# First block's y normalised from SBUF, and eight weight decodes moved into the feed-forward

## The chip, the cores and the metric

The kernel runs on one core of one Trainium2 chip. The metric is device time in microseconds for one execution of the whole program. TensorE's instructions are shown as PE (matmul) and PEld (weight load), VectorE's as DVE, ScalarE's as ACT, GpSimd's as POOL. SP is the engine that issues the transfers.

## The reference

Three layers in a row, all in float32 at the interface. `B, H, S, D = 4, 8, 576, 64`, so there are 2304 tokens of 512 values.

```python
scores = scale * q @ k.T                    # causal by blocks of 64
attn = softmax(scores); x = attn @ v        # [4, 576, 512]

h = relu(x @ w_in); u, v = halves(h)        # 512 + 512 columns
v_n = (v - mean) / sqrt(var + 1e-6)
v_s = einsum('ts,bsd->btd', w_spatial, v_n) + b_spatial
y = (u * v_s) @ w_out                       # [4, 576, 512]

yn = (y - mean(y)) / sqrt(var(y) + 1e-6) * g_ln
out = y + relu(yn @ w_ch1) @ w_ch2          # 512 -> 2048 -> 512
```

The weights come as float64 bits and are turned into float32 on the chip.

## The kernel before, in words

The kernel has four stages. Attention comes first, with the `w_in` products woven in. Then comes the stage this study is about, here called the spatial stage, from about 283 to 434 us. The feed-forward (`w_ch1`, `w_ch2`) follows, to the end.

**Spatial stage.** `order` is a list written out by hand: 16 steps ("s", n) and 18 steps ("y", t). A step s is `spatial(n)`: for one batch and 128 of the 512 features, 28 matmuls of 288 columns into PSUM (`sps`), two multiplications by u on DVE (`gf`, L753), the split of the next operand (ACT L737, DVE L738 and L739), and then `gate`, which splits the gated values into a high part (ACT L761) and a low part (POOL L762). A step y is `y_tile(t)`: 12 matmuls of 512 columns give 128 rows of y in PSUM (`by`), ACT copies them into `ys` (L774, two buffers), and SP stores them to DRAM as `y_d` (L775). The order is s0 to s4, y0 to y3, s5 to s8, y4 to y8, s9 to s12, y9 to y12, s13 to s15, y13 to y17.

**Weights.** `jobs` holds 48 jobs while the stage runs: 32 of `w_ch1` and 16 of the first half of `w_ch2` (`w2a`). The 16 of the second half (`w2b`) are added after it. A job is one load of 256 KB into a `raw` buffer (L661, five buffers), one ACT instruction (L87) and two DVE instructions (L88, L89). `decode_jobs` runs two jobs after each s, one after each y, and four at the end of each step of the feed-forward. The ACT instruction and the first DVE one are pinned behind what was traced before them on their engine.

**The first block's y.** The feed-forward takes 768 rows (six tiles) at a time. `prepare_y(0)` loads the six tiles of `y_d` back into `yn` (L703, two buffers), takes their statistics on DVE (`normalize`: L111, L113, L115), the power on POOL (L116), scales in place on DVE (L117), turns each tile with four transposes on PE (L709) and copies them into `yT` on ACT (L711). `operands` then makes the differences `ts` (L824, three buffers) and the split operands of the up product. `STEPS` says after which s how many pieces of these two generators are traced. The up product of the first step of the feed-forward (`first = up(0)`, matmuls `hps`, L902) is begun between the last y tiles.

**Order on the engines.** Each engine, and SP, runs its instructions in order and waits at the head of its queue. That order is made when the program is built, by a scheduler that reckons with a simulated timeline; `keep_in_program_order` pins an instruction.

Of the kernel before, what the change touches and what calls it, by code (L numbers as in the profile page):

```python
# [8 lines left out]
F32 = mybir.dt.float32  # L9
F32R = mybir.dt.float32r  # L10
U32 = mybir.dt.uint32
AF = mybir.ActivationFunctionType
ALU = mybir.AluOpType
# [3 lines left out]

PLAN = {'mm': 3, 'sc': 3, 'tr': 2, 'D': 2, 'hi0': 'v', 'hi1': 's', 'klo0': 'g', 'klo1': 'g', 'qlo0': 'g', 'qlo1': 'g', 'xm0': 'g', 'xm1': 'g', 'xh0': 'g', 'xh1': 'g', 'xl0': 'g', 'xl1': 'g', 'dm': 'g', 'dh': 'g', 'ev0': 3, 'ev1': 2, 'rate': 24500.0, 'vrb': 3, 'ds': 2, 'dy': 1, 'raw': 5, 'yn': 2, 'ts': 3, 'ring': 8, 'wt': 2, 'cb': 1, 'hq': 8, 'packed': 4, 'plain': 3, 'pre': 8, 'py': 10, 'pyn': 4, 'dn0': 2, 'dnn': 4, 'vl': 'v', 'pace': 3, 'wd': 7, 'tl0': 'v', 'tl1': 'v', 'xe': 's', 'pt': 6, 'dstart': 8}  # L20


def f32(ap):
# [9 lines left out]
def tile_kernel(  # L33
# [12 lines left out]
    nc = tc.nc  # L46

    def E(k, p=None):
        k = PLAN[k if p is None else k + ("0" if p < 4 else "1")]
        return {"v": nc.vector, "g": nc.gpsimd, "s": nc.scalar}[k]  # L50

    def cp(k, p, out, src):
        e = PLAN[k if p is None else k + ("0" if p < 4 else "1")]
        if e == "v":
# [6 lines left out]
    KD = w_in.shape[1]  # L61
    DM = 128 * KD
# [3 lines left out]
    NT = NB * S  # L66
# [39 lines left out]
        MM(out_ps, lhsT=a[0], rhs=b[1], start=False, stop=False)  # L106
        MM(out_ps, lhsT=a[1], rhs=b[0], start=False, stop=last)  # L107

    def normalize(pool, x, rows=128, here=lambda ins: ins):
        st = pool.tile([128, 6], F32, tag="st", name="st")  # L110
        here(nc.vector.bn_stats(st[:rows], x[:rows]))  # L111
        mv = pool.tile([128, 2], F32, tag="mv", name="mv")
        nc.vector.bn_aggr(mv[:rows], st[:rows])  # L113
        rs = pool.tile([128, 1], F32, tag="rs", name="rs")
        nc.vector.tensor_scalar(rs[:rows], mv[:rows, 1:2], 1e-6, None, op0=ALU.add)  # L115
        nc.gpsimd.tensor_tensor(rs[:rows], rs[:rows], nhalf[:rows], op=ALU.pow)  # L116
        return lambda: nc.vector.tensor_scalar(  # L117
            x[:rows], x[:rows], mv[:rows, 0:1], rs[:rows], op0=ALU.subtract, op1=ALU.mult
        )


# [3 lines left out]
    at = tc.alloc_tile_pool(name="at", bufs=2, side="right")  # L125
    p_mm = tc.alloc_tile_pool(name="p_mm", bufs=PLAN["mm"], space=PSUM, side="left")
    p_sc = tc.alloc_tile_pool(name="p_sc", bufs=PLAN["sc"], space=PSUM, side="right")
    p_tr = tc.alloc_tile_pool(name="p_tr", bufs=PLAN["tr"], space=PSUM, side="right")

# [4 lines left out]

    PACKED = PLAN['packed']
    nat = {}
# [27 lines left out]
    idn = const.tile([128, 128], F32, name="idn")  # L164
# [6 lines left out]
    g_sb = const.tile([128, KD], F32, name="g_sb")  # L171
# [327 lines left out]
    def chain(*gens):  # L499
        for g in gens:  # L500
            if g is not None:
                yield from g
# [8 lines left out]
    D = PLAN['D']  # L511
    for u in range(NS + 8):
        p, i = divmod(u, NU)
# [24 lines left out]
        else:  # L538
            b, k = divmod(u, NU * NP)
# [102 lines left out]
    fy = tc.alloc_tile_pool(name="fy", bufs=2, side="left", reuse_waits="tile")  # L642
    fb = tc.alloc_tile_pool(name="fb", bufs=1, side="left", reuse_waits="tile")
    p_h = tc.alloc_tile_pool(name="p_h", bufs=2, space=PSUM, side="left", reuse_waits="tile")
# [5 lines left out]
    jobs = []  # L650
# [12 lines left out]

    done = [0]

    def decode_jobs(k):
        for _ in range(k):
            i = done[0]
            if i == len(jobs):
                return  # L670
            done[0] += 1
            if i not in raws:
                fetch_raw()
            raw = raws.pop(i)
            m = dc.tile([128, 256], F32, tag="dm", name="dm")
            decode(raw, m, raw[:, :, 0], jobs[i][1], tc.keep_in_program_order)
            fetch_raw()
# [9 lines left out]
    NTB = 6  # L687
    BLK = NTB * 128
    HB = BLK // 2
    NBLK = NT // BLK  # L690
    of = out.rearrange("b s d -> (b s) d")
    yT = fy.tile([128, KD, BLK], F32, name="yT", bufs=1)

    def prepare_y(blk):
        if blk >= NBLK:
            return
        yn_t = {}

        def fetch(t):
            if t < NTB:  # L700
                r0 = blk * BLK + 128 * t
                yn_t[t] = fy.tile([128, DM], F32, tag="yn", name="yn", bufs=PLAN["yn"])
                nc.sync.dma_start(out=yn_t[t], in_=y_d[r0:r0 + 128, :])  # L703

        def flip(t):
            yn = yn_t.pop(t)
            tr = p_h.tile([128, 512], F32, tag="h", name="ytr")
            for kc in range(KD):
                nc.tensor.transpose(tr[:, 128 * kc:128 * kc + 128], yn[:, 128 * kc:128 * kc + 128], idn)  # L709
            for kc in range(KD):  # L710
                nc.scalar.activation(  # L711
                    yT[:, kc, 128 * t:128 * t + 128], tr[:, 128 * kc:128 * kc + 128], AF.Copy, scale=g_sb[:, kc:kc + 1]
                )
            fetch(t + 2)

        fetch(0)
        fetch(1)
        yield
        for t in range(NTB):
            scale = normalize(fy, yn_t[t], here=tc.keep_in_program_order) if blk else normalize(fy, yn_t[t])  # L720
            yield
            scale()
            yield
            if t > 0:
                flip(t - 1)
                yield
        flip(NTB - 1)
        yield

# [35 lines left out]

    split_vn(0)

    def y_tile(t):
        c0 = 128 * (t % 9)
        ps = p_by.tile([128, DM], F32, tag="by", name="by")  # L770
        for kc in range(KF):
            mm3(ps, [g[:, kc, c0:c0 + 128] for g in gt], [w[:, kc, :] for w in wo], kc == 0, kc == KF - 1)
        ys = fy.tile([128, DM], F32, tag="ys", name="ys")
        nc.scalar.copy(ys, ps)  # L774
        nc.sync.dma_start(out=y_d[128 * t:128 * t + 128, :], in_=ys)  # L775

    seq = []
    for b in range(NB):
        seq += [("s", KF * b + fc) for fc in range(KF)]
        t0 = 9 * (b // 2) + (0 if b % 2 == 0 else 4)  # L780
        ys = [("y", t) for t in range(t0, t0 + (4 if b % 2 == 0 else 5))]
# [30 lines left out]
    def operands(first=False):  # L812


        b11, b12, b21, b22 = (yT[:, 2 * i:2 * i + 2, HB * k:HB * k + HB] for i in range(2) for k in range(2))
        t1, t2, t3 = (fb.tile([128, KD // 2, HB], F32, tag="ts", name="ts", bufs=3) for _ in range(3))

        def put(i, src):
            pool = fb if i in (0, 2, 6) else fr if i == 4 else fl
            b_t[i] = [pool.tile([128, KD // 2, HB], F32R, tag=f"b{i}{x}", name=f"b{i}{x}") for x in "hl"]  # L820
            split(src, *b_t[i], "s", "v" if i % 2 else "g")

        def sub(out, x, y):
            nc.vector.tensor_tensor(out, x, y, op=ALU.subtract)  # L824

        put(0, b11)
        yield
        put(2, b21)
        if first:
            yield  # L830
            put(6, b22)
            yield
        sub(t1, b12, b11)
        sub(t2, b22, t1)
        yield
        if first:
            sub(t3, b22, b12)
            yield
        put(1, t2)
        if not first:  # L840
            sub(t3, b22, b12)
            yield
        put(3, t3)
        sub(t2, b21, t2)
        yield
        put(5, t2)
        yield
        put(4, t1)
        yield
        if not first:  # L850
            put(6, b22)
            yield
# [117 lines left out]
        nc.sync.dma_start(out=of[r0:r0 + 128, :], in_=yr)  # L970


    STEPS = {6: 1, 7: 2, 8: 2, 9: 3, 10: 3, 11: 3, 12: 3, 13: 2, 14: 3, 15: 2}
    ahead = chain(prepare_y(0), operands(True))
    gate = None
    for kind, n in order:
        if kind == "s":
            gate = spatial(n)
            if n % (2 * KF):
                gate()  # L980
                gate = None
            decode_jobs(PLAN['ds'])
            for _ in range(STEPS.get(n, 0)):
                next(ahead)
            if n == NB * KF - 1:
                p_b1.release()
                ss.release()
                fl = tc.alloc_tile_pool(name="fl", bufs=1, side="left", reuse_waits="tile")
                for _ in range(2):
                    next(ahead)  # L990
                weights(0)
                first = up(0)
        else:
            y_tile(n)
            decode_jobs(PLAN['dy'])
            if n >= NT // 128 - 4 and n < NT // 128 - 1:
                next(first)
        if gate is not None and (kind == "y" or n == 0):
            gate()
            gate = None  # L1000
# [17 lines left out]
    for n, (blk, m) in enumerate(pairs):  # L1018
# [18 lines left out]
        for k in (2, 1, 2, 2, 1, 2, 2):  # L1037
# [3 lines left out]
            for _ in range(k):  # L1041
                t = next(lower)
# [3 lines left out]
        for _ in upper:  # L1046
            pass
        del h_t[n]
        decode_jobs(PLAN["dnn"])
        for i in range(2):  # L1050
            if n + 1 < len(pairs):
# [67 lines left out]
```

## Time and profile before

| | us |
|---|---|
| median of 3 runs | 823.11 (822.58 to 824.65) |
| the profiled execution, its own time | 824.04 |
| its span in the profile | 822.3 |
| PE busy in the span | 791.5 (96%) |
| DVE busy | 519.7 (63%) |
| chain that ended last: share of PE, of DMA, of DVE | 75%, 9%, 8% |

The span is what the trace covers; the 1.7 us beside it lie ahead of the first and behind the last instruction shown. PE is busy nearly always, so what can be won lies where PE sits idle or runs at a lower clock. In the tables a row names the line of the kernel, the engine, the operation, and output<-input by the names of the program.

### The profile page before, as it was taken

Reading aid. Unit: us, or ns where it says so; the run is one execution under the profiler, and the core shown is the slowest. Engines: PE = TensorE matmul, PEld = TensorE weight load, DVE = VectorE, ACT = ScalarE, POOL = GpSimd, SP = SyncE. Lnnn points to the kernel's source line nnn. Section 1 sums busy time; section 2 is a strip of 40 time slices with the busy share of each in tenths; the row PEclk is TensorE's granted clock in tenths of the full one; section 3 lists DMA queues with packets and bytes.
Section 4 is the critical chain, followed back from the end, with each engine's and each line's share of the span. In section 5 each row is a group of like instructions: output and inputs, shape, how many; then the busy total and the mean of one; then the engine's idle time right before and its main releaser. Section 6 shows DMA issues by size and latency. Waiting matters only on the chain.

```text
span 822.3 us, 13272 instructions
## 1 busy us (share of the span) xinstructions
PE 791.5 (96%) x4480; PEld 669.7 (81%) x4480; DVE 519.7 (63%) x1179; ACT 423.9 (52%) x1071; POOL 440.2 (54%) x429
## 2 busy tenths in 40 slices
PE   7899999999999999899889999999999999999998
PEld 4567788768877889888768988898889888988986
DVE  5857654664565276656696578578556659555533
ACT  4688677666755454345554465464345445434331
POOL 4889646654553243214367545587555469445531
PEclk9999999999999999999999999999999999999999
DMA  8745535445241568778531122204000002100002
GB/s 243 199 125 160 157 123 161 137 128 156 86 153 55 162 211 274 236 255 253 203 131 65 52 90 81 61 1 154 1 13 27 14 1 75 67 1 1 1 1 77
DMA packets 54551, 90.24 MB, mean 110 GB/s; under 512 B 6866, under 2 KB 17234, under 8 KB 54484
## 3 DMA queue, kind: packets, MB, share of 16 engines
q1 hardware_dynamic: 54484, 89.40, 35.3%
q8 instruction: 35, 0.57, 0.3%
q14 instruction: 32, 0.26, 0.1%
HBM read 70.43 MB, written 18.95 MB: 109 GB/s over the span
## 4 chain that ended last, share of the span: by engine, by line
PE 75%; DMA 9%; DVE 8%; ACT 3%; SPq 2%; issue 2%; POOL 1%; ACTq 0%; DVEq 0%; POOLq 0%
PE hps L902 20%; PE o L105 8%; PE o L107 8%; PE o L106 8%; PE pv L385 6%; PE tr L332 5%; PE sc L259 3%; PE ups L105 2%; DMA raw<-in_w_in_dram 2%; PE ups L107 2%; PE ups L106 2%; DMA raw<-in_w_ch_dram 2%; DMA yn<-y_d 2%; PE vps L105 1%; PE vps L106 1%
## 5 line engine op out<-in xcount | busy, mean ns | idle before, releaser
L101 POOL TENSOR_TENSOR a<-s,a 128x256 fp32r<-128x256 f32 x96 | 77.4, 811 | 79.1 <-ACT a L96 79.1
L106 PE MATMUL o<-w,h 128*128 128x512 f32 x288 | 112.9, 393 | 0.0
L274 DVE CUSTOM_DVE_ANT_0 p<-sc,mask 128x256 f32<-128x256 f32 (+4 forms) x160 | 73.8, 472 | 56.5 <-PE tr L332 17.5
L105 PE MATMUL o<-w,h 128*128 128x512 f32 x288 | 107.7, 398 | 0.7 <-ACT h L894 0.7
L908 DVE TENSOR_TENSOR c<-hps,c 128x384 f32<-128x384 f32 x120 | 66.6, 555 | 65.4 <-PE hps L902 63.4
L281 ACT ACTIVATE p<-p,nm 128x384 f32<-128x384 f32 (+3 forms) x144 | 83.8, 583 | 32.7 <-DVE nm L274 30.0
L107 PE MATMUL o<-w,h 128*128 128x512 f32 x288 | 97.7, 397 | 1.1 <-DVE h L895 1.1
L101 POOL TENSOR_TENSOR a<-w,a 128x256 fp32r<-128x256 f32 x72 | 63.8, 888 | 40.8 <-ACT a L96 36.7
L96 ACT CAST a<-s 128x256 fp32r<-128x256 f32 x96 | 38.4, 404 | 86.4 <-PE hps L902 78.2
L332 PE MATMUL tr<-idn,p 128*128 128x128 f32 (+1 forms) x400 | 70.2, 287 | 6.1 <-DVE pH L323 5.7
L323 DVE COPY pH<-tr 128x512 f32<-128x512 f32 (+1 forms) x88 | 49.5, 572 | 25.7 <-PE tr L332 25.6
L332 PEld LDWEIGHTS tr<-idn,p 128*128 128x128 f32 (+1 forms) x400 | 47.7, 143 | 19.3 <-issue 5.7
L105 PEld LDWEIGHTS o<-w,h 128*128 128x128 f32 x288 | 53.8, 188 | 11.6 <-ACT h L894 2.1
L106 PEld LDWEIGHTS o<-w,h 128*128 128x128 f32 x288 | 54.1, 188 | 10.1
L107 PEld LDWEIGHTS o<-w,h 128*128 128x128 f32 x288 | 53.3, 188 | 9.8 <-DVE h L895 2.0
L116 POOL TENSOR_TENSOR rs<-rs,nhalf 128x1 f32<-128x1 f32 x36 | 22.8, 634 | 64.4 <-DVE rs L115 64.1
L199 POOL TENSOR_TENSOR stack<-qkt,stack 64x576 fp32r<-64x576 f32 x24 | 34.2, 1427 | 42.2 <-ACT stack L57 41.5
L895 DVE SCALAR_TENSOR_TENSOR h<-c,h 128x384 fp32r<-128x384 f32 x72 | 49.1, 704 | 1.5 <-ACT h L894 1.5
L762 POOL TENSOR_TENSOR gt<-gf,gt 128x576 fp32r<-128x576 f32 (+1 forms) x17 | 25.5, 1501 | 44.0 <-ACT gt L761 43.9
L87 ACT ACTIVATE dm<-raw 128x256 f32<-128x256 f32 (+1 forms) x76 | 34.4, 473 | 26.6 <-DVE w2b L89 6.4
L259 PE MATMUL sc<-stack 128*128 128x512 f32 (+3 forms) x192 | 45.3, 344 | 0.4 <-DVE nm L274 0.2
L96 ACT CAST a<-w 128x256 fp32r<-128x256 f32 x72 | 28.9, 403 | 27.1 <-PE hps L902 27.0
(171 smaller groups left out, 2236.6 us busy)
## 6 DMA issues: line engine op xcount, KB each, us to landing
raw<-in_w_ch_dram SPq DMA_DIRECT2D x64, 256.0 KB
qkt<-in_qk_dram SPq DMA_DIRECT2D x112, 144.0 KB
vt<-in_v_dram SPq DMA_DIRECT2D x16, 320.0 KB
rb<-r_d SPq DMA_DIRECT2D x32, 144.0 KB
u_d<-ur SPq DMA_DIRECT2D x16, 288.0 KB
us<-u_d SPq DMA_DIRECT2D x16, 288.0 KB
y_d<-ys SPq DMA_DIRECT2D x18, 256.0 KB
yn<-y_d SPq DMA_DIRECT2D x18, 256.0 KB
```

Of the source, the lines that this page charges most:

```text
L96: nc.scalar.copy(hi, src)
L101: {"v": nc.vector, "g": nc.gpsimd}[low].tensor_tensor(lo, src, f32(hi), op=ALU.subtract)
L105: MM(out_ps, lhsT=a[0], rhs=b[0], start=first, stop=False)
L106: MM(out_ps, lhsT=a[0], rhs=b[1], start=False, stop=False)
L107: MM(out_ps, lhsT=a[1], rhs=b[0], start=False, stop=last)
L259: MM(s_ps[:, :nn], lhsT=st[:, j, i, q], rhs=st[:, j, 2, 0:nn], start=(i == 0), stop=(i == 1))
L274: nc.vector.tensor_tensor_reduce(pt[:, o:o + n], s_ps[:, :n], m, -0.125, 3e38, ALU.add, ALU.min, nm[:, i:i + 1])
L281: nc.scalar.activation(pt[:, :n], pt[:, :n], AF.Exp, bias=nm[:, 0:1], scale=-1.0, accum_out=sm[:, col:col + 1])
L323: nc.vector.tensor_copy(out, src)
L332: nc.tensor.transpose(tr[:w, o:o + 128], pt[:, 128 * kc:128 * kc + w], idn)
L902: MM(ps, lhsT=a[x], rhs=b[y], start=not more and kc == 0 and k == 0, stop=kc == KD // 2 - 1 and k == 2, skip_group_check=True,)
L908: nc.vector.tensor_tensor(out, ps, x, op=ALU.add)
```

## The change

Three edits, all around the first block.

1. `y_tile` normalises the first six tiles itself: after the copy `ys` and its store, `normalize` reads `ys` and writes a `yn` tile. The six loads from `y_d` go. `flip_y` (the transposes and the copies into `yT`) runs for tile t after y tile t+1, or after the next s.
2. The copies `ys` of tiles 0 to 12 lie in the three buffers of the differences (`ts`); tiles 13 to 17 keep the two old ones.
3. `decode_jobs` stops at 40 jobs in the spatial stage, so the last 8 jobs of `w2a` run in the feed-forward with the 16 of `w2b`. The rate there goes from 4 to 5 jobs per step.

`STEPS` now counts the pieces of `operands` alone: one after each of s11 to s15. Before, the first three of them were traced after s14, the next two after s15.

```diff
-PLAN = {... 'dnn': 4, ...}
+PLAN = {... 'dnn': 5, ...}
-    def normalize(pool, x, rows=128, here=lambda ins: ins):
+    def normalize(pool, x, rows=128, here=lambda ins: ins, out=None):
...
-            x[:rows], x[:rows], mv[:rows, 0:1], rs[:rows], op0=ALU.subtract, op1=ALU.mult
+            (x if out is None else out)[:rows], x[:rows], mv[:rows, 0:1], rs[:rows],
+            op0=ALU.subtract, op1=ALU.mult,
...
-    def decode_jobs(k):
+    def decode_jobs(k, last=1 << 30):
...
-            if i == len(jobs):
+            if i == min(len(jobs), last):
...
+    def flip_y(t, yn):
+        tr = p_h.tile([128, 512], F32, tag="h", name="ytr")
+        for kc in range(KD):
+            nc.tensor.transpose(tr[:, 128 * kc:128 * kc + 128], yn[:, 128 * kc:128 * kc + 128], idn)
+        for kc in range(KD):
+            nc.scalar.activation(
+                yT[:, kc, 128 * t:128 * t + 128], tr[:, 128 * kc:128 * kc + 128], AF.Copy, scale=g_sb[:, kc:kc + 1]
+            )
...
+    flips = []
     def y_tile(t):
...
-        ys = fy.tile([128, DM], F32, tag="ys", name="ys")
+        if t < NT // 128 - 5:
+            ys = fb.tile([128, KD // 2 * HB], F32, tag="ts", name="ys", bufs=3)[:, :DM]
+        else:
+            ys = fy.tile([128, DM], F32, tag="ys", name="ys")
         nc.scalar.copy(ys, ps)
         nc.sync.dma_start(out=y_d[128 * t:128 * t + 128, :], in_=ys)
+        if t < NTB:
+            yn = fy.tile([128, DM], F32, tag="yn", name="yn", bufs=PLAN["yn"])
+            normalize(fy, ys, out=yn)()
+            flips.append((t, yn))
...
-    STEPS = {6: 1, 7: 2, 8: 2, 9: 3, 10: 3, 11: 3, 12: 3, 13: 2, 14: 3, 15: 2}
-    ahead = chain(prepare_y(0), operands(True))
+    STEPS = {11: 1, 12: 1, 13: 1, 14: 1, 15: 1}
+    ahead = operands(True)
...
-            decode_jobs(PLAN['ds'])
+            decode_jobs(PLAN['ds'], 40)
+            while flips:
+                flip_y(*flips.pop(0))
...
             y_tile(n)
-            decode_jobs(PLAN['dy'])
+            decode_jobs(PLAN['dy'], 40)
+            while len(flips) > 1:
+                flip_y(*flips.pop(0))
```

## Rows read from the trace of the kernel before

**Rows 1.** Windows, two feed-forward steps: busy us (instructions), PEclk, DMA share, GB/s.
```profile
core 0: us, PE busy (x) PEld busy (x) DVE busy (x) ACT busy (x) POOL busy (x), PEclk, DMA share, GB/s
501.50:517.80 16.30, 16.30 (x85) 14.58 (x84) 13.32 (x27) 8.78 (x23) 8.99 (x11) 1.00 0.28 78
517.80:534.00 16.20, 16.03 (x81) 13.76 (x81) 8.62 (x14) 7.66 (x21) 7.08 (x8) 1.00 0.12 37
```
**Rows 2.** Windows over the spatial stage, as in rows 1.
```profile
309.00:337.00 28.00, 28.00 (x179) 26.08 (x178) 17.69 (x44) 12.64 (x26) 6.61 (x4) 1.00 0.90 288
337.00:347.00 10.00, 7.93 (x53) 6.98 (x53) 7.70 (x19) 3.46 (x8) 2.98 (x3) 1.00 0.64 193
347.00:372.00 25.00, 24.21 (x142) 21.50 (x142) 14.29 (x39) 12.15 (x29) 6.04 (x4) 1.00 0.79 251
372.00:404.00 32.00, 28.66 (x178) 25.42 (x177) 20.18 (x50) 14.53 (x36) 11.11 (x9) 1.00 0.65 208
404.00:434.50 30.50, 26.66 (x126) 21.65 (x125) 26.54 (x44) 17.38 (x44) 18.47 (x16) 0.94 0.52 177
```
**Rows 3.** Waits of PE, 308 to 440 us: us in total, times, longest.
```profile
PE sps L105 <- DVE gf L753: 3.1, 4, 1.4
PE ytr L709 <- DVE yn L117: 2.7, 2, 1.7
PE hps L902 <- ACT a L96: 1.4, 2, 1.2
PE by L105 <- ACT gt L761: 1.2, 1, 1.2
PE sps L105 <- DVE mv L113: 0.6, 1, 0.6
PE hps L902 <- DVE b1l L101: 0.5, 1, 0.5
```
**Rows 4.** DVE by line, 309 to 404 us: busy, mean ns | idle ahead of it.
```profile
L88 DVE TENSOR_SCALAR raw<-raw 128x256 uint32<-128x256 uint32 x40 | 12.6, 316 | 17.0 <-DMA raw<-in_w_ch_dram 17.0
L111 DVE BATCH_NORM_STATS2 st<-yn 128x6 f32<-128x512 f32 x6 | 4.2, 693 | 9.7 <-DMA yn<-y_d 9.7
L113 DVE BATCH_NORM_AGGREGATE mv<-st 128x2 f32<-128x6 f32 x6 | 1.0, 171 | 0.0
L115 DVE TENSOR_SCALAR rs<-mv 128x1 f32<-128x1 f32 x6 | 0.8, 139 | 0.0
```
**Rows 5.** Timeline, 337 to 401.5 us: start, us, engine, line [idle before <-releaser].
```profile
339.83 0.69 DVE L111 BATCH_NORM_STATS2 st<-yn 128x6 f32<-128x512 f32 x1 [1.24 <-DMA yn<-y_d]
...
341.70 0.37 PE L105 MATMUL sps<-ws,hl 128*128 128x288 f32 x1 [1.40 <-DVE gf L753]
...
386.46 1.87 POOL L101 TENSOR_TENSOR b0l<-yT,b0h 128x768 fp32r<-128x768 f32 x1 [0.19 <-ACT b0h L96]
...
386.51 2.10 DVE L117 TENSOR_SCALAR yn<-yn,mv,rs 128x512 f32<-128x512 f32 x1
...
400.30 0.55 POOL L116 TENSOR_TENSOR rs<-rs,nhalf 128x1 f32<-128x1 f32 x1 [6.28 <-DVE rs L115]
```
**Rows 6.** The chain that ended last, in order of time: start us, us, what.
```profile
332.21 4.25 DMA y_d<-ys
```
**Rows 7.** Waits of ACT, 308 to 440 us, as in rows 3.
```profile
ACT ys L774 <- DMA y_d<-ys: 6.4, 2, 3.7
```
**Rows 8.** DVE by line, 404 to 434.5 us.
```profile
L89 DVE SCALAR_TENSOR_TENSOR w2a<-dm,raw 128x256 uint32<-128x256 uint32 x10 | 5.5, 549 | 0.3
L88 DVE TENSOR_SCALAR raw<-raw 128x256 uint32<-128x256 uint32 x9 | 4.2, 471 | 1.4 <-DMA raw<-in_w_ch_dram 1.4
```
**Rows 9.** Windows over the end of the stage, as in rows 1.
```profile
418.00:420.00 2.00, 1.06 (x3) 0.48 (x3) 2.00 (x4) 1.87 (x7) 1.32 (x2) 1.00 0.51 146
420.00:422.00 2.00, 1.47 (x6) 0.97 (x6) 2.00 (x4) 1.02 (x5) 2.00 (x3) 0.78 0.36 118
422.00:424.00 2.00, 2.00 (x6) 1.90 (x7) 2.00 (x3) 2.00 (x6) 2.00 (x2) 0.50 0.31 117
```
**Rows 10.** Tiles yn, ys: duration ns min/median/max, first and last start us.
```profile
L117 DVE TENSOR_SCALAR yn<-yn,mv,rs x18: 529/547/2101, 341.7 to 641.3; 128x512 f32<-128x512 f32 x18
...
L774 ACT COPY ys<-by x18: 567/584/603, 328.1 to 434.2; 128x512 f32<-128x512 f32 x18
```
**Rows 11.** Timeline of PE: first and last of 24 matmuls of y tiles.
```profile
329.23 0.40 PE L105 MATMUL by<-wo,gt 128*128 128x512 f32 x1
...
334.46 0.39 PE L107 MATMUL by<-wo,gt 128*128 128x512 f32 x1
```
**Rows 12.** DVE by line, 434.5 to 530 us.
```profile
L89 DVE SCALAR_TENSOR_TENSOR w2b<-dm,raw 128x256 uint32<-128x256 uint32 x16 | 10.1, 629 | 0.6
L88 DVE TENSOR_SCALAR raw<-raw 128x256 uint32<-128x256 uint32 x16 | 7.9, 492 | 0.0
```

More of the change, by code (lines that the diff above doesn't have):

```diff
@@ L16 @@
 DRAM = bass.MemoryType.DRAM
-PLAN = {'mm': 3, 'sc': 3, 'tr': 2, 'D': 2, 'hi0': 'v', 'hi1': 's', 'klo0': 'g', 'klo1': 'g', 'qlo0': 'g', 'qlo1': 'g', 'xm0': 'g', 'xm1': 'g', 'xh0': 'g', 'xh1': 'g', 'xl0': 'g', 'xl1': 'g', 'dm': 'g', 'dh': 'g', 'ev0': 3, 'ev1': 2, 'rate': 24500.0, 'vrb': 3, 'ds': 2, 'dy': 1, 'raw': 5, 'yn': 2, 'ts': 3, 'ring': 8, 'wt': 2, 'cb': 1, 'hq': 8, 'packed': 4, 'plain': 3, 'pre': 8, 'py': 10, 'pyn': 4, 'dn0': 2, 'dnn': 4, 'vl': 'v', 'pace': 3, 'wd': 7, 'tl0': 'v', 'tl1': 'v', 'xe': 's', 'pt': 6, 'dstart': 8}
+PLAN = {'mm': 3, 'sc': 3, 'tr': 2, 'D': 2, 'hi0': 'v', 'hi1': 's', 'klo0': 'g', 'klo1': 'g', 'qlo0': 'g', 'qlo1': 'g', 'xm0': 'g', 'xm1': 'g', 'xh0': 'g', 'xh1': 'g', 'xl0': 'g', 'xl1': 'g', 'dm': 'g', 'dh': 'g', 'ev0': 3, 'ev1': 2, 'rate': 24500.0, 'vrb': 3, 'ds': 2, 'dy': 1, 'raw': 5, 'yn': 2, 'ts': 3, 'ring': 8, 'wt': 2, 'cb': 1, 'hq': 8, 'packed': 4, 'plain': 3, 'pre': 8, 'py': 10, 'pyn': 4, 'dn0': 2, 'dnn': 5, 'vl': 'v', 'pace': 3, 'wd': 7, 'tl0': 'v', 'tl1': 'v', 'xe': 's', 'pt': 6, 'dstart': 8}
 def f32(ap):
@@ L705, in flip @@
         def flip(t):
[L706 to L713, printed above, removed]
+            flip_y(t, yn_t.pop(t))
             fetch(t + 2)
@@ L719, in prepare_y @@
         for t in range(NTB):
-            scale = normalize(fy, yn_t[t], here=tc.keep_in_program_order) if blk else normalize(fy, yn_t[t])
+            scale = normalize(fy, yn_t[t], here=tc.keep_in_program_order)
             yield
```

## The prediction

> **What bounds the kernel now.** I first read the page: PE is busy 96% of the span, so only stretches in which PE idles or is clocked down can give anything back. The table of windows comes next, to find them. In the feed-forward there is next to nothing: a step of 16.30 us shows PE busy 16.30 [rows 1]. The spatial stage is where it lacks: 2.07 us idle in 337 to 347, 0.79 in 347 to 372, 3.34 in 372 to 404, 3.84 in 404 to 434.5 [rows 2], 10.0 us together. In the last of these the granted clock is below 1 as well, 0.94 on average; that is 0.06 x 30.5 = 1.8 us more. So about 11.8 us is all that could come back.
>
> The list of PE's waits says who ended this idle time [rows 3]: DVE, nearly always (the product `gf`, the scaled `yn`, the statistics), and ACT at the end. But DVE is busy just 14 to 20 us in those longer windows up to 404 us. It is late, not full. DVE's own idle time shows why [rows 4]: 17.0 us in front of the first decode instruction, waiting for its weights, and 9.7 us in front of the statistics, waiting for the reload of y. Both stand at the head of an in-order queue, and what PE needs stands behind. The timeline has the pattern: statistics start at 339.83 after a wait for the reload, and PE gets its `gf` with 1.40 us of idle time at 341.70 [rows 5]. After 404 us it is another story: DVE is busy 26.54 of 30.5 us, so there it is full.
>
> **The reload goes (edit 1).** It removes six loads of 256 KB and six waits at the head of DVE's queue, 9.7 us of DVE idle time. What of that PE felt: the longest wait for `gf`, 1.4, the two for `yn`, 2.7, the one for the aggregate, 0.6 [rows 3]. That makes 4.7 us, my term, **-4.7**. Lower bound of the gain 1.0: the next at DVE's head may be a decode that waits for its load instead. Upper bound 6.4, with the three other `gf` waits (3.1 - 1.4 = 1.7) as backlog of the same stalls. SP is rid of six issues that wait for a store to land, and the transfers of 1.57 MB; at the 208 GB/s of 372 to 404 [rows 2] that is 7.6 us of the transfer engines' time, which makes weight loads earlier. I give it nothing of its own, since PE doesn't wait for these loads directly; it stands against the lower bound.
>
> The work itself stays: six statistics, aggregates, additions and scales on DVE, six powers on POOL, 24 transposes, 24 ACT copies. It moves ahead, next to the y tiles.
>
> **The copies in `ts` (edit 2).** Three buffers where there were two, and each is now held until its store has landed and its scale has run. The differences are first written after s14 and need the buffers of tiles 10 to 12 back. A store took 4.25 us from issue to landing in the chain [rows 6]; the cover is s13 and s14, 56 matmuls, by 32 us for 178 PE instructions [rows 2] about 10 us, an estimate. So 0; without that cover it would be up to 4.25 us. ACT waited 6.4 us for stores to give back one of its two buffers [rows 7]; a third can only help, and I give it 0, since no wait of PE hangs on it in the list [rows 3].
>
> **Eight decodes leave the stage (edit 3).** Per job 0.549 + 0.471 us of DVE [rows 8], eight jobs 8.2 us, out of the 26.5 us that DVE is busy from 404 us on. ACT loses eight short instructions with them. The pieces of `operands` also start three s steps earlier, so the high parts are off ACT before the rush. What is to be won is the 3.84 us of idle time and the 1.8 us of clock. The windows show the clock falling to 0.50, the lower of its two levels (1.2 GHz), at 422 to 424, behind two windows with PE busy 1.06 and 1.47 of 2 us [rows 9]. Without that hole it need not fall. Not all goes: the weights' split for the first up product (ACT, POOL) still has to follow the last s. Bounds 0 and 5.7; I take **-4.0**, nearer the upper end, because the DVE time taken away (8.2) is twice the idle time.
>
> **The new waits: six flips.** PE now gets transposes of tile t behind y tile t+1. The chain from the last matmul of tile t is copy 0.58 [rows 10], statistics 0.69, aggregate 0.17, addition 0.14 [rows 4], power 0.55 [rows 5], scale 0.55 at the median, 2.10 at most [rows 10]: 2.7 to 4.2 us. The cover is the next y tile, 12 matmuls at (334.46 - 329.23)/23 = 0.227 us each [rows 11], 2.7 us. Tiles 0, 1, 2 and 4 have just that; tiles 3 and 5 also have a spatial step in front. So four flips with an excess of 0 to 1.5 us, 0 to 6.0 in all, more when ACT or DVE is held ahead of the copy or the statistics. DVE's decodes wait 17.0 us for weights [rows 4], and a statistics behind one of them delays PE. I take 0.5 each for four, **+2.0**; most scales in the trace ran at the short time, but queues are never quite empty.
>
> The scale's long time has a cause that the rows show: the one at 386.51 took 2.10 us while POOL worked on a subtraction from 386.46 for 1.87 [rows 5]. The Trainium skill, page "SBUF — State Buffer", section "Who interferes with whom", says that a tensor_scalar on VectorE can take a mode that uses the pair of ports it shares with GpSimd, and that whoever comes second is then held for the whole of the other's instruction. The trace agrees at that place. The move puts the scales beside the y tiles, where the gate's subtraction runs on POOL; by the rule each could meet one, and by the rows' median none does. By the median the four flips cost nothing, by the maximum 6.0.
>
> **The feed-forward takes the eight jobs.** There a job costs 0.629 + 0.492 = 1.12 us of DVE [rows 12]. The steps with decodes had four and get five; the fifth step had none and gets four. The fullest step had DVE busy 13.32 of 16.30 us and would come to 14.4; the fifth 8.62 and would come to 13.1 [rows 1]. PE was fully busy with DVE at 13.3, so the cover holds. **+0.5**; bounds 0 and 9.0, all eight on PE's path if the two PSUM banks of the up product gave no slack. The weights are in time: jobs 40 to 43 are split at the end of step 1 (counted from 0) and are decoded at the end of step 0, one step ahead.
>
> **Sum.** -4.7 - 4.0 + 2.0 + 0.5 = -6.2 us. From the profiled execution's 824.04 that makes 817.8. The median shown is 0.93 lower, so 816.9 for a median.
>
> **Rivals.**
> A. *The weights' loads take the reload's place.* DVE's queue still holds decodes that waited 17.0 us. If the next instruction at its head is one of those, the first term shrinks to -1.0, the second, which doesn't hang on it, to -2, and the flips cost 2: with 0.5 that is -0.5, so 822.6. For it: decodes are pinned in order. Against it: the reload's own transfers and SP's blocked issues go, so weights come earlier; and of the 17.0 us at most the 1.7 us of the other `gf` waits reached PE [rows 3, 4].
> B. *PE waits for its flips: slower.* One mechanism: the chain behind each y tile is longer than the tile that covers it. The gain ahead of it is 8.7 less 0.5, so it decides from 8.2/6 = 1.4 us per flip on, all six. At 2.1 us each (the whole length of the slow scale) 12.6 come on: +4.4, 827.5. For it: scales ran up to 2.10, and the decodes' waits can hold a statistics. Against it: only four flips are without a spatial step, and the scheduler can put a flip later.
> C. *The feed-forward pays.* Half of the 9.0 us shows: -8.7 + 2 + 4.5 = -2.2, 820.9. Against it: PE was full at 82% of DVE.
> D. *The whole stage closes up.* All 11.8 us and no flip waits: 811.3. Against it: the tail of the stage has a true chain through `gf`, `gt` and the last tiles.
>
> **How the numbers follow.** A run of this kernel tells a change from none at about 0.3%, 2.5 us. Chances: forecast 0.57 (its own range 813 to 820), A 0.15, B 0.12, C 0.08, D 0.08. Faster by over 0.3% takes the forecast, D, and a little of C and A: 0.69. Slower takes B and a small part of the mixed cases, 0.12; the rest, 0.19, is no difference. The range for 8 in 10 leaves out most of B and the edge of D: 811.5 to 823.5.
>
> **What would show it.** Right: no wait of DVE for y before the feed-forward; PE busy over 31 of 32 us in 372 to 404; the granted clock at 1.00 through the end of the stage; the first up products a few us earlier; feed-forward steps still 16.2 to 16.3 us. Wrong: a row "PE ytr waits for DVE yn" above 4 us (B), the idle time in front of the decodes grown by the same 9.7 us (A), steps of the first block above 17 us (C), or differences that wait for a store (edit 2).

## The result, and the profile after

| | before | changed |
|---|---|---|
| median, us | 822.85 (821.84 to 824.65, 4 runs) | 813.24 (812.78 to 814.33, 4 runs) |
| ratio of the runs, 95% interval | | 0.9891 (0.9874 to 0.9908) |
| profiled execution, own time / span | 824.04 / 822.3 | 812.78 / 811.0 |

The kernel got faster by 9.6 us between medians; 816.9 had been forecast, 811.5 to 823.5 as the range. First the page of the changed kernel, its span and PE's line:

```profile
span 811.0 us, 13252 instructions
...
PE 787.5 (97%) x4480; PEld 670.4 (83%) x4480; DVE 525.9 (65%) x1179; ACT 423.6 (52%) x1071; POOL 441.9 (54%) x429
```

Where in the span it came from is seen with two marks, the last matmul of `ups` and the matmuls of `o`. These are rows of tile `ups` and tile `o`, with the first and last start at the end of the numbers. Before:

```profile
L107 PE MATMUL ups<-xT,win x128: 289/294/380, 108.1 to 309.1; 128*128 128x288 f32 x128
...
L105 PE MATMUL o<-w,h x288: 387/395/501, 436.5 to 817.7; 128*128 128x512 f32 x144
```

Changed:

```profile
L107 PE MATMUL ups<-xT,win x128: 289/294/380, 107.3 to 308.4; 128*128 128x288 f32 x128
...
L105 PE MATMUL o<-w,h x288: 387/395/505, 424.9 to 806.3; 128*128 128x512 f32 x144
```

From the one mark to the other the spatial stage took 436.5 - 309.1 = 127.4 us and now takes 116.5: 10.9 us less. The feed-forward, first to last `o`, took 381.2 and takes 381.4. So nearly all of the 11.3 us between the two spans lies in the stage, and the eight extra decodes cost the feed-forward next to nothing. (These two executions lie further apart than the medians, 11.3 us against 9.6.)

The windows of the changed kernel, as in [rows 2]; the last one ends where `o` begins:

```profile
337.00:347.00 10.00, 7.48 (x55) 6.81 (x54) 8.75 (x18) 5.08 (x13) 4.55 (x4) 1.00 0.55 168
347.00:372.00 25.00, 25.00 (x147) 22.27 (x146) 17.12 (x45) 14.06 (x35) 8.40 (x6) 1.00 0.77 239
372.00:404.00 32.00, 31.76 (x199) 29.15 (x198) 23.70 (x47) 13.68 (x29) 9.84 (x6) 1.00 0.79 254
404.00:424.90 20.90, 20.49 (x105) 17.64 (x104) 14.31 (x20) 12.78 (x28) 15.14 (x15) 1.00 0.21 73
```

In 337 to 404 PE idles 2.52 + 0 + 0.24 = 2.8 us where it idled 2.07 + 0.79 + 3.34 = 6.2 [rows 2]. In the last window it idles 0.4 us at a granted clock of 1.00, where the end of the stage had 3.8 us and a clock of 0.94 [rows 2]. DVE is busy 14.3 of 20.9 us there and no longer full. PE's waits, 308 to 440 us, as in [rows 3], and DVE by line, 309 to 404 us, as in [rows 4]:

```profile
PE sps L105 <- DVE gf L756: 1.7, 2, 1.5
PE ytr L698 <- DVE yn L117: 0.6, 1, 0.6
PE sps L107 <- DVE low L741: 0.5, 1, 0.5
PE hps L915 <- ACT b4h L96: 0.4, 1, 0.4
```
```profile
L88 DVE TENSOR_SCALAR raw<-raw 128x256 uint32<-128x256 uint32 x40 | 18.3, 457 | 11.6 <-DMA raw<-in_w_ch_dram 11.6
...
L111 DVE BATCH_NORM_STATS2 st<-ys 128x6 f32<-128x512 f32 x6 | 4.1, 686 | 0.2 <-ACT ys L783 0.2
L117 DVE TENSOR_SCALAR yn<-ys,mv,rs 128x512 f32<-128x512 f32 x6 | 3.3, 546 | 3.3 <-POOL rs L116 3.2
```

The statistics' wait is gone (9.7 to 0.2 us), and the wait for weights fell too, from 17.0 to 11.6: the reload's wait did not turn into one for weights. Against that, the decodes' first instruction (L88) is busy 18.3 us where it was 12.6 [rows 4], 457 ns on average against 316. The flips cost PE 0.6 us in one place.

### The profile page after: what moved, and what is told of

Same layout as the page of the kernel before. It is cut to its first block, busy times and chain, and to the rows that moved or that the text cites. A ratio compares the mean times of both kernels' runs of the same rounds, so it can differ in the third digit from the quotient of the medians.

```text
span 811.0 us, 13252 instructions
## 1 busy us (share of the span) xinstructions
PE 787.5 (97%) x4480; PEld 670.4 (83%) x4480; DVE 525.9 (65%) x1179; ACT 423.6 (52%) x1071; POOL 441.9 (54%) x429
## 4 chain that ended last, share of the span: by engine, by line
PE 78%; DVE 8%; DMA 6%; ACT 3%; issue 2%; SPq 2%; POOL 1%; DVEq 0%; ACTq 0%; POOLq 0%
PE hps L915 20%; PE o L105 8%; PE o L107 8%; PE o L106 7%; PE pv L386 6%; PE tr L333 5%; PE sc L260 4%; DMA raw<-in_w_ch_dram 2%; PE ups L105 2%; PE ups L107 2%; PE ups L106 2%; DMA raw<-in_w_in_dram 2%; PE by L107 2%; PE by L105 2%; PE by L106 2%
```

## The experiments

Twelve kernels. Each was timed beside the kernel before on its own chip, so ratios are what is compared. A ratio's interval is some 1.0 to 1.9 us to either side. "Stage" is the time between the two marks in the profiled execution. That is one execution, and it need not be a typical one: it was the slowest of six in late_operands and the fastest of six in spare_loads_read and spare_loads_tiny.

| run | median us | ratio, 95% interval | stage us |
|---|---|---|---|
| changed kernel | 813.24 | 0.9891 (0.9874 to 0.9908) | 116.5 |
| without_decode_move | 815.12 | 0.9903 (0.9887 to 0.9918) | 119.1 |
| decode_move_alone | 822.50 | 0.9992 (0.9978 to 1.0005) | 125.4 |
| reload_kept | 821.88 | 0.9980 (0.9966 to 0.9993) | 125.8 |
| two_copy_buffers | 814.57 | 0.9899 (0.9882 to 0.9915) | 117.5 |
| late_operands | 815.42 | 0.9917 (0.9897 to 0.9936) | 119.3 |
| spare_loads | 818.69 | 0.9947 (0.9923 to 0.9970) | 122.0 |
| spare_loads_read | 815.95 | 0.9928 (0.9906 to 0.9951) | 118.5 |
| reload_five_buffers | 823.20 | 1.0005 (0.9988 to 1.0021) | 127.1 |
| spare_loads_no_wait | 811.93 | 0.9875 (0.9853 to 0.9896) | 116.5 |
| spare_loads_tiny | 815.09 | 0.9905 (0.9889 to 0.9922) | 117.7 |
| operands_pinned | 811.42 | 0.9862 (0.9844 to 0.9880) | 114.8 |
| flips_uncovered | 812.59 | 0.9893 (0.9871 to 0.9915) | 116.3 |

**First question: which of the three edits.** Four runs undo or do one alone.

without_decode_move:
```diff
-PLAN = {... 'dnn': 5, ...}
+PLAN = {... 'dnn': 4, ...}
-            decode_jobs(PLAN['ds'], 40)
+            decode_jobs(PLAN['ds'], 48)
...
-            decode_jobs(PLAN['dy'], 40)
+            decode_jobs(PLAN['dy'], 48)
```


> The changed kernel with edit 3 undone: all 48 jobs run in the spatial stage, four per step in the feed-forward. Theory (two separate parts: the reload held DVE's queue before 404 us, the decodes filled DVE after it): the end of the stage gets its idle time back, 4 to 5 us, so 817 to 818. Rival 'early operands' (the end of the stage got faster because the differences and operands were made earlier, not because decodes left): 814 or less. Rival 'decodes alone': 820 to 823.

It gave 815.12. The end of the stage did not get its 4 to 5 us back: 0.9903 against 0.9891 is 1.0 us by ratios, 1.9 by medians, with overlapping intervals, and the stage of the profiled execution is 2.6 us longer. The theory of two separate parts is wrong in its second half, and the rival "early operands" (814 or less) is closer. With all 48 jobs in the stage PE idles 2.4 us from 404 us to the first `o`, and the granted clock stays at 1.00:

```profile
404.00:427.10 23.10, 20.73 (x103) 17.25 (x103) 19.64 (x33) 14.98 (x35) 14.48 (x15) 1.00 0.44 148
```

decode_move_alone, the kernel before with
```diff
-PLAN = {... 'dnn': 4, ...}
+PLAN = {... 'dnn': 5, ...}
-    def decode_jobs(k):
+    def decode_jobs(k, last=1 << 30):
...
-            if i == len(jobs):
+            if i == min(len(jobs), last):
...
-            decode_jobs(PLAN['ds'])
+            decode_jobs(PLAN['ds'], 40)
...
-            decode_jobs(PLAN['dy'])
+            decode_jobs(PLAN['dy'], 40)
```


> The kernel before with edit 3 alone: 40 jobs in the stage, the rest at five per step of the feed-forward; y is still loaded back. Theory of two separate parts: 4 to 5 us faster than before, 818 to 819. Rival 'early operands': under 1 us, about 822. Rival 'decodes alone': near the changed kernel, 813 to 815.

It gave 822.50, a ratio whose interval holds 1; the stage of the profiled execution is 2.0 us shorter than before. With eight jobs fewer PE still idles at the end of the stage: 3.3 of 31.5 us in the window 404 to 435.5, against 4.5 of 32.5 in the same part of the kernel before (404 to 436.5). DVE is busy 24.6 of the 31.5 us and no longer full, so its fullness is not what most of PE's idle time came from. One thing differs: the granted clock is 1.00, where it was 0.95 in that part.

```profile
404.00:435.50 31.50, 28.21 (x146) 23.53 (x146) 24.61 (x34) 18.45 (x42) 19.15 (x17) 1.00 0.37 126
```

reload_kept, the same with the copies in `ts` as well (edit 2):
```diff
-        ys = fy.tile([128, DM], F32, tag="ys", name="ys")
+        if t < NT // 128 - 5:
+            ys = fb.tile([128, KD // 2 * HB], F32, tag="ts", name="ys", bufs=3)[:, :DM]
+        else:
+            ys = fy.tile([128, DM], F32, tag="ys", name="ys")
```


> Edits 2 and 3 without edit 1: copies of y in the three buffers of the differences and eight decodes moved, but y of the first block is still loaded back and normalised as before. Theory of two parts: what the reload cost stays, so 818 to 819, as with the decode move alone, the buffers giving at most 1 us. Rival 'the buffers matter': 815 to 816.

821.88, and not the 818 to 819 of two parts. From here to the changed kernel only edit 1 is missing, with its places in `STEPS`, and that step is 0.9980 to 0.9891: 7.3 of 822.85 us. The windows of reload_kept, from its first mark to 404 us and from there to the first `o`, say where:

```profile
308.00:404.00 96.00, 90.11 (x558) 81.48 (x557) 62.00 (x154) 44.45 (x100) 26.17 (x20) 1.00 0.77 243
404.00:433.80 29.80, 26.49 (x123) 21.45 (x122) 21.64 (x25) 15.38 (x37) 19.00 (x17) 0.94 0.33 115
```

Ahead of 404 us PE idles 5.9 us, against 2.8 in the changed kernel. Behind it PE idles 3.3 us, and the clock costs 0.06 x 29.8 = 1.8 us more, against 0.4 us at 1.00. So edit 1 works in both parts of the stage, and the clock is low here although the eight decodes are gone.

two_copy_buffers, the changed kernel with the four lines of edit 2 back to the one old line:
```diff
-        if t < NT // 128 - 5:
-            ys = fb.tile([128, KD // 2 * HB], F32, tag="ts", name="ys", bufs=3)[:, :DM]
-        else:
-            ys = fy.tile([128, DM], F32, tag="ys", name="ys")
+        ys = fy.tile([128, DM], F32, tag="ys", name="ys")
```


> The changed kernel with edit 2 undone: the copies of y lie in the two old buffers, each now held by its store and its scale. Theory: the buffers are worth little, 813 to 814.5. Rival 'the buffers matter' (with two, the copy of the third tile waits for a store, its PSUM bank is not free and PE waits): 816 to 819, with a wait of PE's y matmuls for the copy above 2 us.

814.57: 0.7 us by ratios, within the intervals; PE waits 0.8 us for the copy there. So the buffers are worth little, as expected (813 to 814.5).

**Second question: what in edit 1.** The timeline has a hint. The first difference (`ts`) starts at 408.51 in the kernel before and at 409.46 with the decodes moved alone; in the changed kernel it starts at 396.57, 11.9 us earlier, or 11.2 counted from the first mark (three kernels, a row each):

```profile
408.51 0.95 DVE L824 TENSOR_TENSOR ts<-yT 128x768 f32<-128x768 f32 x1
```
```profile
409.46 0.95 DVE L824 TENSOR_TENSOR ts<-yT 128x768 f32<-128x768 f32 x1
```
```profile
396.57 0.96 DVE L837 TENSOR_TENSOR ts<-yT 128x768 f32<-128x768 f32 x1 [0.37 <-DMA y_d<-ys]
```

What the late start does is seen in the kernel before. Two differences take over 2 us each on DVE, the last products `gf` stand behind them, ACT can split `gf` into `gt` only then, and PE waits 1.20 us (timeline of the kernel before):

```profile
409.75 2.26 DVE L824 TENSOR_TENSOR ts<-yT,ts 128x768 f32<-128x768 f32 x1
411.93 2.18 DVE L824 TENSOR_TENSOR ts<-yT 128x768 f32<-128x768 f32 x1
...
414.57 0.44 DVE L753 TENSOR_TENSOR gf<-us,sps 128x288 f32<-128x288 f32 x1
...
415.05 0.43 ACT L761 CAST gt<-gf 128x288 fp32r<-128x288 f32 x1 [3.80 <-DVE gf L753]
...
415.53 0.50 PE L105 MATMUL by<-wo,gt 128*128 128x512 f32 x1 [1.20 <-ACT gt L761]
```

late_operands keeps all three edits and traces the operands late again, pinned there; operands_pinned has the same pins at the changed kernel's places. The difference between the two is `STEPS` alone, but for pins on the differences (DVE), which only late_operands has.

late_operands:
```diff
-    STEPS = {11: 1, 12: 1, 13: 1, 14: 1, 15: 1}
+    STEPS = {14: 3, 15: 2}
...
-            split(src, *b_t[i], "s", "v" if i % 2 else "g")
+            hi, lo = b_t[i]
+            here = tc.keep_in_program_order if first else lambda ins: ins
+            here(nc.scalar.copy(hi, src))
+            (nc.vector if i % 2 else nc.gpsimd).tensor_tensor(lo, src, f32(hi), op=ALU.subtract)
...
-            nc.vector.tensor_tensor(out, x, y, op=ALU.subtract)
+            here = tc.keep_in_program_order if first else lambda ins: ins
+            here(nc.vector.tensor_tensor(out, x, y, op=ALU.subtract))
```


> The changed kernel with the five pieces of the operands traced where they were before (three after s14, two after s15) and their copies and differences pinned behind what was traced ahead of them; y is still normalised from its copy and eight decodes still leave the stage. Theory of lateness (most of the gain comes because the first block's y is ready some 35 us sooner, so differences and operands are made ahead of the rush at the end of the stage): 816.5 to 819, with PE idle 3 us or more from 404 us on. Rival 'head of the queue' (DVE no longer stands waiting for the reload): 813 to 814.

operands_pinned:
```diff
-            split(src, *b_t[i], "s", "v" if i % 2 else "g")
+            hi, lo = b_t[i]
+            here = tc.keep_in_program_order if first else lambda ins: ins
+            here(nc.scalar.copy(hi, src))
+            (nc.vector if i % 2 else nc.gpsimd).tensor_tensor(lo, src, f32(hi), op=ALU.subtract)
```


> The changed kernel with the ACT copies of the operands pinned at the places where they are traced (after s11 and later), so that none is run some 40 us ahead and the POOL subtraction behind it doesn't fall on DVE's decodes at 343 us. Theory (the 2.5 us that PE still idles in 337 to 347 come from that subtraction, as two decodes there took 1.54 and 1.96 us instead of 0.28): 811.5 to 812.5. Rival (PE's wait there has another cause, or moves on): 813 to 814.

815.42 and 811.42, 0.9917 and 0.9862, intervals apart: operands that are late in this way cost 4.5 us. Against the changed kernel alone late_operands is just 2.1 us up, less than expected, because its pins also help ahead of 404 us, where PE idles 1.0 us and not 2.8. The window from 404 us to the first `o` in late_operands, then in operands_pinned, then PE's longest wait of late_operands, from its list of waits:

```profile
404.00:428.60 24.60, 21.23 (x86) 17.13 (x85) 17.48 (x18) 11.44 (x25) 19.26 (x16) 0.86 0.18 65
```
```profile
404.00:424.30 20.30, 19.46 (x96) 16.45 (x96) 14.23 (x18) 12.64 (x28) 15.79 (x15) 1.00 0.23 73
```
```profile
PE by L107 <- POOL gt L765: 2.5, 1, 2.5
```

With late operands PE idles 3.4 us and the granted clock averages 0.86; with early ones 0.8 us at 1.00. Idle time and a lower clock, as in the kernel before [rows 2, 9], are back although the eight decodes are gone. But this is not the hole of the kernel before. Pinned late, three subtractions for the operands stand in POOL's queue ahead of the last `gt`, and PE waits for POOL (timeline of late_operands):

```profile
401.79 1.88 POOL L837 TENSOR_TENSOR b0l<-yT,b0h 128x768 fp32r<-128x768 f32 x1
...
403.61 2.60 POOL L837 TENSOR_TENSOR b2l<-yT,b2h 128x768 fp32r<-128x768 f32 x1
...
406.18 2.55 POOL L837 TENSOR_TENSOR b6l<-yT,b6h 128x768 fp32r<-128x768 f32 x1
...
408.69 2.44 POOL L765 TENSOR_TENSOR gt<-gf,gt 128x288 fp32r<-128x288 f32 x2
...
410.25 1.22 PE L107 MATMUL by<-wo,gt 128*128 128x512 f32 x2 [2.47 <-POOL gt L765]
```

In the kernel before two of these three subtractions had started by 388.29 us. Also, the first difference of late_operands starts 9 us later than that of operands_pinned (403.40 against 394.51), not 12. So 4.5 us shows that late operands can cost as much; it is not a measure of what lateness cost in the kernel before.

operands_pinned also answers its own question. In the changed kernel two decodes near 343 us were slow, each while POOL was at work (timeline of the changed kernel):

```profile
341.14 1.43 POOL L765 TENSOR_TENSOR gt<-gf,gt 128x576 fp32r<-128x576 f32 x1 [0.46 <-ACT gt L764]
341.19 1.54 DVE L88 TENSOR_SCALAR raw<-raw 128x256 uint32<-128x256 uint32 x1
...
343.23 2.03 POOL L101 TENSOR_TENSOR b0l<-yT,b0h 128x768 fp32r<-128x768 f32 x1 [0.66 <-ACT b0h L96]
343.45 1.96 DVE L88 TENSOR_SCALAR raw<-raw 128x256 uint32<-128x256 uint32 x1
```

With the operands pinned behind s11 the first stays slow (1.53 us at 342.05), beside `gt`. The second takes 0.28 us, PE's wait of 1.5 us for `gf` is gone, and PE is busy 9.05 of the 10 us from 337 on, not 7.48 (operands_pinned, its timeline and its window):

```profile
344.31 0.28 DVE L88 TENSOR_SCALAR raw<-raw 128x256 uint32<-128x256 uint32 x1
```
```profile
337.00:347.00 10.00, 9.05 (x68) 8.59 (x67) 8.19 (x21) 6.00 (x19) 2.52 (x3) 1.00 0.53 169
```

811.42 lies just below the expected 811.5 to 812.5 and is the fastest of the versions that do the kernel's work and no more; its interval overlaps that of the changed kernel, so the 1.8 us between the medians are not clear of noise.

**Third question: the rest of edit 1.** Taken as they stand, 4.5 of 7.3 us would leave some 3 for the waits at the head of DVE's queue, for SP's, or for the bytes. Four runs add spare loads to the changed kernel, and one gives the old reload more buffers. The spare loads are traced at the old places of the reload (s6 to s13) and write into the two old copy buffers, which are free then; nothing uses what they bring. SP issues those of spare_loads from 333 to 368 us, where it issued the old reload from 334 to 407, so they are like the old loads and not the same.

spare_loads, core of the edit:
```diff
+        def fetch(t):
+            if t < NTB:
+                sp[t] = fy.tile([128, DM], F32, tag="ys", name="sp")
+                nc.sync.dma_start(out=sp[t], in_=y_d[128 * t:128 * t + 128, :])
...
+    SPARE = {6: 1, 7: 2, 8: 2, 9: 3, 10: 3, 11: 3, 12: 3, 13: 2}
+    spare = spare_loads(False)
```


> The changed kernel plus the six loads of y as before, into the two old copy buffers, which nothing reads: the transfers and SP's waits for the stores are back, DVE waits for none of them. Theory of lateness and rival 'head of the queue' alike: within 1 us of the changed kernel, 813 to 814.5. Rival 'traffic' (the 1.57 MB and SP's blocked issues delayed the weights): 816 or more, with DVE's waits for weights back at 15 us or more.

818.69, 4.6 us by ratios above the changed kernel, with runs from 814.08 to 821.19. The rival "traffic" had the time right; of the waits for weights it expected 15 us or more, and the profile has 14.1. The list of waits of SP (325 to 410 us), that of DVE (309 to 404) and the timeline show how:

```profile
SPq L777 <- DMA y_d<-ys: 13.1, 5, 4.3
```
```profile
DVE raw L88 <- DMA raw<-in_w_ch_dram: 14.1, 9, 4.7
```
```profile
382.65 0.29 DVE L88 TENSOR_SCALAR raw<-raw 128x256 uint32<-128x256 uint32 x1 [3.45 <-DMA raw<-in_w_ch_dram]
...
383.90 0.40 PE L105 MATMUL sps<-ws,hl 128*128 128x288 f32 x1 [3.00 <-DVE gf L756]
```

SP stands 13.1 us waiting for y's stores to land, the weight loads behind it go out late (the 28th of the stage at 367.16 us, in the changed kernel at 363.05), the first DVE instruction of a decode waits 3.45 us for one, and PE gets its `gf` 3.00 us late. No one reads the spare loads.

spare_loads_read, the same with statistics taken on DVE:
```diff
+            if stats:
+                st = fy.tile([128, 6], F32, tag="st", name="st")
+                nc.vector.bn_stats(st, sp[t])
...
+    spare = spare_loads(True)
```


> As the run with spare loads, and DVE takes the statistics of each loaded tile, which nothing uses: the wait at the head of DVE's queue is back (and 6 x 0.69 = 4.1 us of DVE work more), but y is ready early. Rival 'head of the queue': 3 to 5 us above the run with spare loads, 816.5 to 819. Theory of lateness: 0.5 to 1.5 us above it, 814 to 815.5.

815.95, not above the run without the reading but 1.6 us below it by ratios (intervals overlap). "Head of the queue" expected 3 to 5 us more. DVE's wait for the spare loads was 3.4 us in the profile, not the old 9.7, so the wait was brought back in part only. So reading the loads adds no price that shows. This run's interval just overlaps that of the changed kernel, so the price of the loads is seen clear of noise in spare_loads alone.

spare_loads_no_wait and spare_loads_tiny take the two halves apart:
```diff
-                nc.sync.dma_start(out=sp[t], in_=y_d[128 * t:128 * t + 128, :])
+                nc.sync.dma_start(out=sp[t].bitcast(U32), in_=wo32[:, t % KF, 0:DM])
```


> The changed kernel plus six spare loads of 256 KB that nothing reads, at the same places, but from w_out, which lies ready in DRAM: the bytes are there, and SP waits for no store. Theory 'SP waits' (the reload cost mostly because SP stood in its queue until a y store had landed, and the weight loads behind it were issued late): at most 1.5 us above the changed kernel, 813 to 815. Rival 'bytes': as the run with spare loads of y, 816.5 to 819.


```diff
-                nc.sync.dma_start(out=sp[t], in_=y_d[128 * t:128 * t + 128, :])
+                nc.sync.dma_start(out=sp[t][:, 0:4], in_=y_d[128 * t:128 * t + 128, 0:4])
```


> As the run with spare loads of y, but each of the six takes 16 bytes per partition (2 KB in place of 256): SP waits for the stores as before, and there is next to nothing to move. Theory 'SP waits': most of the loss stays, 816 to 819. Rival 'bytes': 813 to 814.5.

The bytes without a wait cost nothing: 811.93, 0.9875, in reach of the changed kernel's interval. (These loads were also issued earlier, from 322 to 339 us, so the bytes were not tried at the later places.) The waits without bytes: 815.09, between the two expectations, 1.2 us up by ratios, intervals overlapping, with SP waiting 9.6 us for stores. So "bytes" alone shows no cost where it was tried, and "SP waits" is not shown alone; the two together cost 4.6 us, whose interval lies clear of the changed kernel's.

reload_five_buffers, the kernel before with the reload asked for early:
```diff
-                yn_t[t] = fy.tile([128, DM], F32, tag="yn", name="yn", bufs=PLAN["yn"])
+                if blk or t in (3, 4):
+                    yn_t[t] = fy.tile([128, DM], F32, tag="yn", name="yn", bufs=PLAN["yn"])
+                else:
+                    yn_t[t] = fb.tile([128, KD // 2 * HB], F32, tag="ts", name="yn", bufs=3)[:, :DM]
...
-            fetch(t + 2)
+            for i in (t + 2,) if blk else (4, 5) if t == 0 else ():
+                fetch(i)
...
-        fetch(0)
-        fetch(1)
+        for t in range(2 if blk else 4):
+            fetch(t)
```


> The kernel before with the reload kept but asked for early: five buffers (three of them those of the differences), tiles 0 to 3 loaded at s6, tiles 4 and 5 three steps later, so that the statistics need not wait for two buffers to come free. Places of the pieces as before, decodes as before. Theory of lateness: DVE's waits for the reload fall from 9.7 us to under 4, but y is ready only a little sooner, so 820 to 822. Rival 'head of the queue': 817 to 819.

823.20, no gain. It failed as a test of the DVE wait: that fell only from 9.7 to 8.9 us. It does say that more buffers alone don't mend the reload.

flips_uncovered:
```diff
-            while len(flips) > 1:
+            while len(flips) > 0:
```


> The changed kernel with each flip traced right behind its own y tile, without the next tile as cover. Rival B of the prediction (PE waits for the chain of copy, statistics, power and scale, 2.7 to 4.2 us each): up to 6 x 2.7 = 16 us more if nothing else stands between; the scheduler may put matmuls of other steps there. Theory (the chain is covered, and without cover it costs): 815 to 822, with PE's wait for the scaled y at 3 us or more. Rival 'the scheduler finds other cover': 813 to 814.

812.59: no cost. PE shows no wait for the scaled y at all in this run. But the edit hardly moved the flips: the first four start at 332.9, 334.9, 337.4 and 340.6 us, in the changed kernel at 333.2, 335.3, 338.4 and 341.5. The scheduler kept other matmuls ahead of them, so the run does not price a flip without cover.

## Why the prediction was right, and in which terms it was not

The direction, the stage and the range were right: PE's idle time in the spatial stage was what came back, the feed-forward held, and 813.24 lies inside 811.5 to 823.5. The sum of -6.2 was too small. Edit 1 was put at -4.7 + 2.0 = -2.7 and measured -7.3; edit 3 was put at -4.0 + 0.5 = -3.5 and measured about -1. These two misses go opposite ways and cancel in part, so that the total came as near as it did is partly luck.

- **The reload, -4.7.** Edit 1 as a whole is worth 7.3 us (reload_kept to changed). The prediction counted only the waits that PE showed behind DVE's stalls; ahead of 404 us PE's idle time fell by 3.4 us from the kernel before. What it left out is what edit 1 does behind 404 us, where PE's idle time fell from 3.3 to 0.4 us and the clock rose from 0.94 to 1.00 (reload_kept to changed). The first block's y is ready sooner, which the prediction had put down under the decodes. Rival A (weights take the reload's place) is refuted: that wait fell, 17.0 to 11.6 us.
- **The eight decodes, -4.0.** This is the step that failed: "nearer the upper end, because the DVE time taken away (8.2) is twice the idle time". The move measures 0.7 us alone and 1.0 on top of the others by ratios, each within the noise; the profiled stages say 2.0 and 2.6. DVE's fullness was not what PE mostly waited for: in decode_move_alone DVE had room and PE idled 3.3 us still. In the kernel before the waits there go back to the differences and operands of the first block, which began 12 us later than in the changed kernel. That this lateness is the cause is read from the timeline and fits without_decode_move; late_operands against operands_pinned (4.5 us) shows that late operands can cost as much, through another wait. The 1.8 us of lowered clock do not hang on the decodes either: the clock is 1.00 with them in without_decode_move and 0.94 without them in reload_kept. With late operands it is 0.86 in late_operands but 1.00 in decode_move_alone, so what brought it down stays open.
- **The flips, +2.0.** Measured 0.6 us of PE's wait in the profile. The chain was sized rightly (scales 546 ns on average), but the order the scheduler made puts other matmuls in front. Rival B did not come.
- **The scales and the shared ports.** All six scales took their short time. The Trainium skill, page "SBUF — State Buffer", section "Who interferes with whom", says that GpSimd and an instruction of VectorE that uses both pairs of ports lock each other out, so that the one that comes second is blocked for the whole of the other's instruction. The trace agrees in two places more: the decodes' first DVE instruction, also a tensor_scalar, took 1.54 and 1.96 us beside POOL's subtractions, and 0.28 without. So the move did meet POOL, at a place that the prediction had not looked at, and that cost part of the 2.5 us that PE still idled in 337 to 347.
- **The buffers, 0.** Measured 0.7 us, within the interval. DVE's differences do wait for stores now, 1.4 us in the profile, which the prediction had named as a sign of being wrong, but PE waits for none of that.
- **The feed-forward, +0.5.** Measured 0.2 in the profile. Rival C did not come.
- **The transfers, given nothing of their own.** Bytes alone, where they were tried: nothing. Bytes behind SP's waits for stores cost 4.6 us when added to the changed kernel. The prediction gave SP's six blocked issues nothing because PE does not wait for these loads directly; it should have asked what is queued behind them on SP.

Taken in the order edit 3, edit 2, edit 1, the ratios give 0.7, 1.0 and 7.3 us. They add up to the 9.0 of 0.9891 by construction.

**What stays open.** How the 7.3 us of edit 1 divide between the earlier operands, DVE's wait for the reload and SP's wait for the stores. In the kernel before, SP's list has just 2.1 us under waits of the reload for a store, against 13.1 in spare_loads, so that run shows what such loads can cost, not what they did cost. A reload with DVE's wait taken away and SP's kept was not obtained, nor one run that brings back the late operands of the kernel before and nothing else.

## What to carry to other kernels

Where an engine is full for a stretch, ask first when its work could have begun, and only then how much of it can be moved elsewhere: here 8.2 us of DVE work taken out gave about 1 us by ratios, while the edit that, among other things, had the stretch's input ready 12 us earlier gave 7.3. A load that must wait for a store can hold what stands behind it on its issuing queue: six such loads cost 4.6 us in spare_loads, and as many bytes without the wait, issued earlier, cost nothing. So count what stands behind a load as well as its bytes. And work that a scheduler may float can land beside an engine it slows: a decode took 1.96 us beside a floated subtraction and 0.28 without it.

## What the runs showed that was not expected

In late_operands one hole cost more than its length. PE did nothing from 407.8 to 410.25 us, while it waited for `gt`. The granted clock was 1.00 in the window with the hole and 0.50 right behind it, the lower of its two levels (1.2 GHz), with PE busy again:

```profile
408.00:410.00 2.00, 0.00 (x0) 0.00 (x0) 2.00 (x2) 0.00 (x0) 2.00 (x2) 1.00 0.00 0
410.00:412.00 2.00, 1.50 (x3) 0.78 (x4) 1.97 (x4) 0.92 (x2) 1.13 (x2) 0.50 0.00 0
412.00:414.00 2.00, 2.00 (x5) 1.55 (x6) 1.29 (x3) 2.00 (x5) 0.00 (x0) 0.50 0.70 262
```

Executions of one kernel scatter by more than many of the differences here: 817.38 to 823.62 in reload_kept (12 runs), 814.08 to 821.19 in spare_loads (8 runs), and 811.88 to 817.37 in flips_uncovered (6 runs), which loads no y of the first block back.
